# Attention, MoE and soft MoE on one core: q and k of batches 1 to 3 loaded in 32x32 blocks and transposed on VectorE

## Chip, core and metric

One core of a Trainium2 chip runs the kernel alone. The metric is the time of one execution in device microseconds (us), the median of several runs. Lower is better.

## What is computed

Three layers follow one another, all in float32: causal attention, a dense layer with a gated ReLU6, and a soft mixture of experts.

```python
batch, n_heads, seq, head_dim = 4, 12, 448, 64          # q, k, v

def _attn_ref(q, k, v):
    scores = np.matmul(q, k.transpose(0, 1, 3, 2)) / np.sqrt(64)
    scores = np.where(np.triu(np.ones((448, 448), bool), k=1), -1e9, scores)
    scores = scores - np.max(scores, axis=-1, keepdims=True)
    attn = np.exp(scores)
    attn = attn / (np.sum(attn, axis=-1, keepdims=True) + 1e-09)
    return np.matmul(attn, v)

def _moe_ref(x, w_in, w_out):                           # 1792 x 768, 768 x 2048, 2048 x 768
    h = x @ w_in
    return (h * np.clip(h + 3.0, 0.0, 6.0) / 6.0) @ w_out

def _moe2_ref(x, phi, w1, w2):                          # 8 experts of 4 slots, w1 8 x 768 x 1024
    logits = x @ phi
    d = softmax of logits over the 1792 tokens
    slot_input = (d.T @ x).reshape(8, 4, 768)
    slot_out[e] = np.maximum(slot_input[e] @ w1[e], 0.0) @ w2[e]
    return (softmax of logits over the 32 slots) @ slot_out
```

w_in and w_out arrive as 64-bit floats and are turned into 32-bit ones on the chip.

## The kernel before

**A planner writes the order.** Every piece of work is a `Step` with an engine (or several to choose from), a cost in us, the steps it depends on, the buffers it uses and a due time `prio`. `Schedule.run` places the steps one after the other: on each engine the step that can start first goes first, and among those that can start within `WAIT` of it the one with the smallest `prio`. Instructions are issued in that order, so each engine works through a fixed list. All DMAs are issued by SP (L398), so SP's list is the order of the transfers too. A buffer comes from a named pool and is given back after the last step that uses it. The constants in `TU` (L20) are due times, costs and buffer counts. Where the planner expects TensorE to idle it puts in filler matmuls (L382), whose result nobody reads.

**Attention** (L403) runs over 24 pairs of heads, six for each of the four batches. For a pair, two DMAs bring q into `qr` (112 partitions, four rows of 64 for each head) and two bring k into `kr`; there is one `qr` and one `kr` (`Q` is 1). Four TensorE transposes for each of them (L431, `tr`) put the head dimension onto the partitions, 448 columns in a PSUM buffer `t`. ScalarE copies that to `qp` or `kp` as the high part (L401), and VectorE subtracts it from the PSUM value for the low part (L437). From these come the scores with the mask (L453, L459), the row maxima on VectorE (L466), a diagonal matrix of the maxima on VectorE or GpSimd (L476 to L480), the scores again with the maxima taken off (L497, L502), exp on ScalarE (L512), the causal cut on GpSimd (L520), the product with v (L535), the division by the sums (L546 to L548), and a transpose of the result (L556) into `xp`, the input of the MoE. `xp` has two buffers, so batch 2 writes into the one that batch 0's MoE has left.

**The conversion** (`conv`, L573) of w_out (16 blocks, in the first stage) and w_in (16 blocks, while batch 0's MoE runs) loads 768 KB into `raw`, and ScalarE and VectorE put the 32-bit floats together (L577 to L589). The results go through the two `cx` buffers to DRAM (`wf_d`) and, split into high and low part (`wpl`, two buffers, L672 to L677), to `wi_d`. Later batches load them from there.

**The MoE** (L653) goes batch by batch over 16 units. Each unit multiplies `xp` with a block of w_in in 18 matmuls (L691), applies the gate (L696, L698), transposes the result through a PSUM buffer `t` (L705, L710), and from time to time feeds the logits (L720). There are two buffers `t`, and the transposes of attention, conversion and MoE share them.

**The experts** (L998, L1105) stream 50 MB of w1 and w2 through `ring` buffers. These come free in steps: after the conversion (`cv_end`), after attention (`a_end`), and as parts of the MoE end (`b_end` to `m_end`); `RINGS` says how many come at each step. The output is written at the end.

The change touches the attention of batches 1 to 3 up to `qp` and `kp`, and constants of the planner.

Of the kernel before, what the change touches and what calls it, by code (L numbers as in the profile page):

```python
# [9 lines left out]
F32 = mybir.dt.float32  # L10
# [8 lines left out]

TU = {'PO': [0.0, -5.47, -45.9, 12.37], 'TO': [-7.42, -0.39, 42.22, 1.8], 'PB': 0.11, 'AB': -0.28, 'TB': 293.74, 'DUTY': 0.6, 'RINGS': [3, 3, 2, 3, 1, 6, 2, 3], 'LOOK': 0.46, 'FILL': 0.96, 'RAW': 3, 'CA': 1, 'CW': 1, 'S': 2, 'PAIR': 15.8, 'UNIT': 3.58, 'WP0': 12.63, 'WPS': 9.72, 'T0': 82.6, 'L0': 11.83, 'L1': 5.94, 'GP': 244.34, 'TP': 7.98, 'ZP': 104.14, 'UP': -1.93, 'P0': 13.95, 'NQ': 2, 'WAIT': 0.12, 'AHEAD': 1.43, 'LAT': 0.23, 'CX': 2, 'G': 5, 'R': 1, 'VR': 2, 'XT': 2, 'Q': 1, 'AS': 1.42, 'A1': -3.91, 'A2': 3.39, 'A3': 15.18, 'A4': 12.3, 'A5': 11.1, 'A6': 20.26, 'A7': 6.65, 'DG': 2}  # L20

# [16 lines left out]
class Schedule:  # L38
# [4 lines left out]
    LAT = 0.15  # L43
    LATS = {"PE": 0.2, "ACT": 0.15, "DVE": 0.15, "POOL": 0.08, "SP": 0.1}
    LOOK = TU["LOOK"]
    BIAS = {"POOL": TU["PB"], "ACT": TU["AB"]}
    TB = TU["TB"]
# [138 lines left out]
def kernel(  # L186
# [12 lines left out]
    nc = tc.nc  # L199
# [68 lines left out]
    with tc.manual_schedule():  # L268
# [72 lines left out]
        nc.vector.memset(oner.bitcast(F32), 1.0)  # L341
        many(atp, TU["Q"], "qr", [112, QR, 2, DH])
        many(atp, TU["Q"], "kr", [112, QR, 2, DH])
        for t in many(atp, TU["VR"], "vr", [P, 2, NT, VD]):
# [52 lines left out]
        def dma(out, in_):  # L397
            nc.sync.dma_start(out=out, in_=in_)  # L398
# [4 lines left out]
        def attention(i):  # L403
# [7 lines left out]
            hs = slice(2 * hp, 2 * hp + 2)  # L411

            def ld(buf, src):
                for h in range(2):
                    dma(buf.t[:, :, h, :], src[b, 2 * hp + h].rearrange("(r p) d -> p r d", r=QR))

# [6 lines left out]
            for nm, buf, src in (("q", qr, q), ("k", kr, k)):  # L423
                l = sc.load(0.46e6, lambda buf=buf, src=src: ld(buf, src), [], [buf], p0 - 30, 2)
                tp, dst = sc.buf("t"), sc.buf(nm + "p")
                pl[nm] = dst

                def tr(tp=tp, buf=buf):
                    for r in range(QR):
                        x = buf.t[:, r].rearrange("p h d -> p (h d)")  # L430
                        nc.tensor.transpose(tp.t[:, 112 * r:112 * r + 112], x, ident[:112, :112])  # L431

                a = sc.add("PE", 0.5, tr, [l], [tp, buf, dst], p0)
                a.weight = 0.3
                c = sc.add("ACT", 0.58, lambda tp=tp, dst=dst: act_copy(dst.t[:, 0], tp.t[:, :S]), [a], [tp, dst], p0)
                his.append(c)
                los.append(sc.add("DVE", 0.61, lambda tp=tp, dst=dst: nc.vector.tensor_sub(  # L437
                    dst.t[:, 1], tp.t[:, :S], dst.t[:, 0].bitcast(F32)), [c], [tp, dst], p0))
            vl = sc.load(0.46e6, ldv, [], [vr], p0 - 20, 3)
# [4 lines left out]
            for part in (((3, 64), (0, 0)), ((1, 0), (2, 192))):  # L444
# [24 lines left out]

                a = sc.add("PE", 0.95, score, his, [ps, mc_, pl["q"], pl["k"]], P1)  # L470
                a.weight = 0.7
# [11 lines left out]

            d = sc.any([("POOL", 2.6, lambda: diag(nc.gpsimd)), ("DVE", 1.1, lambda: diag(nc.vector))], ms, [mc_, dg], P3)

# [53 lines left out]

            w = sc.add("PE", 2.1, pv, es + [vl], [o, s, vr], P6)  # L540
            w.weight = 0.6
# [31 lines left out]
        def conv(src, out, use, deps, prio, tag):  # L573
            raw, ca, cw = sc.buf("raw"), sc.buf("ca"), sc.buf("cw")
            l = sc.load(0.79e6, lambda: dma(raw.t.rearrange("p k f t -> p k (f t)"), src), [], [raw], prio - 12)
            hw = lambda: raw.t[:, :, :, 1]
            a = sc.add("ACT", 0.91, lambda: nc.scalar.activation(  # L577
                out=ca.t, in_=hw().bitcast(F32), func=ACTF.Copy, scale=2.0 ** -112), [l], [raw, ca], prio)
            c = sc.any([
                ("DVE", 0.74, lambda: nc.vector.tensor_scalar(  # L580
                    out=cw.t, in0=raw.t[:, :, :, 0].bitcast(U32), scalar1=29, scalar2=None,
                    op0=ALU.logical_shift_right)),
                ("ACT", 0.9, lambda: nc.scalar.activation(
                    out=cw.t, in_=raw.t[:, :, :, 0].bitcast(U32), func=ACTF.Copy, scale=LOW, bias=LOWB)),
            ], [l], [raw, cw], prio)
            e = sc.add("DVE", 1.04, lambda: nc.vector.scalar_tensor_tensor(  # L586
                out=cw.t, in0=ca.t.bitcast(U32), scalar=3, in1=cw.t,
                op0=ALU.logical_shift_left, op1=ALU.bitwise_or), [a, c], [ca, cw], prio)
            return sc.add("DVE", 1.06, lambda: nc.vector.scalar_tensor_tensor(  # L589
                out=out().bitcast(U32), in0=hw().bitcast(U32), scalar=0x80000000, in1=cw.t,  # L590
                op0=ALU.bitwise_and, op1=ALU.bitwise_or), [e] + deps, [raw, cw] + use, prio)
# [61 lines left out]
        for b in range(B):  # L653
# [5 lines left out]
            for ft in range(KF):  # L659
# [53 lines left out]

                a = sc.add("PE", 0.45, tr, [gg], [tp, g, gtb], pr - TU["TP"])
                a.weight = 0.35
# [482 lines left out]
```

## Time and profile before

| | us |
|---|---|
| median of 3 runs (687.77 to 694.6) | 690.55 |
| profiled execution, its time | 688.96 |
| profiled execution, its span | 687.2 |

The profile is of one execution on the chip. Its page begins with the busy time of each engine and closes with the groups of instructions and the DMA issues. PE is TensorE, PEld its weight loads, DVE VectorE, ACT ScalarE, POOL GpSimd, SP the engine that issues DMAs. The trace behind the page also answers questions: the busy time of all engines or of one line in stretches of time; the chain of waits, followed back from the last instruction, in order of time; groups of instructions by line and form with their mean duration; the DMA queue in a stretch; SP's own timeline. A share of the DMA engines is the mean busy share of the 16, by the time of their packets, and can go a little over 1 where packets overlap.

### The profile page before, as it was taken

What the parts mean: (1) busy time and instruction counts of PE and PEld (TensorE: products, weight loads), DVE (VectorE), ACT (ScalarE), POOL (GpSimd) and SP (SyncE); (2) the same over time, 40 slices, a digit from 0 to 9 for tenths busy, and PEclk for the clock granted to TensorE, in tenths of its full rate; (3) what the DMA queues carried; (4) which work ended last, traced back from release to release, by engine and by line L of the source; (5) the groups of instructions that cost most, each with busy time, mean ns of one, the idle gap of its engine ahead of it and who ended that gap; (6) DMA issues with size and microseconds to landing.
All of it is one profiled execution on the core that took longest, in us unless ns stands there. A gap on an engine that the chain in (4) does not pass through costs nothing.

```text
span 687.2 us, 16051 instructions
## 1 busy us (share of the span) xinstructions
PE 639.8 (93%) x6810; PEld 493.5 (72%) x6810; DVE 321.0 (47%) x658; ACT 265.6 (39%) x492; POOL 65.9 (10%) x131
## 2 busy tenths in 40 slices
PE   7898999999999999999999999999999999968374
PEld 5776888888888878888887888878698744522133
DVE  6786898878774544233445442123433333111101
ACT  2585665565653323333333233323344312201011
POOL 0231222224130000000000000000000010000000
PEclk7999999999999999999999999999999999996657
DMA  8889789999978935544543534279922399999997
GB/s 207 280 284 282 236 247 329 289 351 331 319 274 284 313 95 147 158 126 121 138 149 97 149 107 138 93 247 346 325 71 92 116 354 385 377 371 334 308 309 225
DMA packets 142614, 161.56 MB, mean 235 GB/s; under 512 B 71632, under 2 KB 113872, under 8 KB 142544
## 3 DMA queue, kind: packets, MB, share of 16 engines
q1 hardware_dynamic: 142544, 160.56, 72.6%
q8 instruction: 53, 0.87, 0.5%
q14 instruction: 17, 0.14, 0.1%
HBM read 129.86 MB, written 30.67 MB: 234 GB/s over the span
## 4 chain that ended last, share of the span: by engine, by line
PE 80%; DMA 12%; SPq 2%; DVE 2%; ACT 2%; issue 1%; ACTq 0%; DVEq 0%
PE ph L691 22%; PE pl L691 12%; PE o L535 7%; PE ps L497 6%; PE t L705 4%; DMA ring<-in_moe_w_dram 4%; PE ps L453 3%; PE t L431 3%; PE t L556 3%; SPq L398 2%; DMA raw<-in_moe_w_out_dram 2%; DMA wos<-in_moe_w_dram 2%; PE t L619 2%; PE ps L459 2%; PE ps L502 2%; PE t L849 2%
## 5 line engine op out<-in xcount | busy, mean ns | idle before, releaser
L691 PE MATMUL ph<-xp,wpl 128*128 128x448 f32 x720 | 157.1, 371 | 0.8 <-DMA wpl<-wi_d 0.8
L691 PEld LDWEIGHTS ph<-xp,wpl 128*128 128x128 f32 x720 | 132.2, 188 | 17.0 <-ACT r L696 2.2
L691 PE MATMUL pl<-xp,wpl 128*128 128x448 f32 x432 | 94.3, 371 | 0.9 <-DMA wpl<-wi_d 0.9
L691 PEld LDWEIGHTS pl<-xp,wpl 128*128 128x128 f32 x432 | 79.5, 188 | 7.9 <-DMA wpl<-wi_d 1.2
L520 POOL TENSOR_SCALAR_AFFINE_SELECT s<-s 128x256 f32<-128x256 f32 x96 | 42.9, 470 | 340.1 <-ACT s L512 287.1
L698 DVE SCALAR_TENSOR_TENSOR g<-r,ph 128x448 f32<-128x448 f32 x40 | 24.8, 621 | 100.7 <-ACT r L696 100.7
L696 ACT ACTIVATE r<-ph,three 128x448 f32<-128x448 f32 x40 | 25.3, 634 | 104.0 <-PE ph L691 104.0
L466 DVE TENSOR_REDUCE mc<-ps 128x2 f32<-128x896 f32 (+1 forms) x96 | 61.4, 682 | 5.8 <-PE ps L459 4.9
L512 ACT ACTIVATE s<-ps 128x896 f32<-128x896 f32 (+2 forms) x72 | 50.2, 732 | 27.2 <-PE ps L502 26.3
L497 PE MATMUL ps<-qp,kp 64*64 64x64 f32 (+3 forms) x576 | 57.5, 306 | 2.0 <-ACT s L512 2.0
L497 PEld LDWEIGHTS ps<-qp,kp 64*128 64x128 f32 (+1 forms) x576 | 41.9, 174 | 17.2 <-issue 8.8
L535 PE MATMUL o<-vr,s 128*64 128x65 f32 (+1 forms) x1536 | 53.6, 224 | 0.0
L535 PEld LDWEIGHTS o<-vr,s 128*64 128x64 f32 (+1 forms) x1536 | 48.6, 137 | 3.6 <-issue 1.0
L710 ACT ACTIVATE gtok<-t 128x384 f32<-128x384 f32 x64 | 31.0, 485 | 29.8 <-PE t L705 29.7
L705 PE MATMUL t<-ident,g 128*128 128x128 f32 (+1 forms) x256 | 39.2, 280 | 0.0
L698 DVE SCALAR_TENSOR_TENSOR g<-r,pl 128x448 f32<-128x448 f32 x24 | 14.9, 620 | 50.5 <-ACT r L696 50.4
L586 DVE SCALAR_TENSOR_TENSOR cw<-ca,cw 128x768 uint32<-128x768 uint32 x32 | 33.3, 1040 | 10.2 <-ACT ca L577 5.2
L577 ACT ACTIVATE ca<-raw 128x768 f32<-128x768 f32 x32 | 29.2, 912 | 21.8 <-DMA raw<-in_moe_w_in_dram 7.3
L696 ACT ACTIVATE r<-pl,three 128x448 f32<-128x448 f32 x24 | 15.2, 634 | 52.6 <-PE pl L691 52.6
L453 PE MATMUL ps<-kp,qp 64*128 64x448 f32 (+1 forms) x192 | 34.6, 362 | 0.7 <-ACT kp L401 0.3
L705 PEld LDWEIGHTS t<-ident,g 128*128 128x128 f32 (+1 forms) x256 | 26.8, 133 | 8.0 <-issue 1.2
L1113 PE MATMUL o<-ring,wos 128*32 128x128 f32 (+1 forms) x248 | 20.4, 449 | 11.5 <-DMA ring<-in_moe_w_dram 11.5
(208 smaller groups left out, 823.1 us busy)
## 6 DMA issues: line engine op xcount, KB each, us to landing
ring<-in_moe_w_dram SPq DMA_DIRECT2D x44, 768.0 KB, 10.9
wpl<-wi_d SPq DMA_DIRECT2D x32, 768.0 KB, 4.4
raw<-in_moe_w_out_dram SPq DMA_DIRECT2D x16, 768.0 KB, 6.0
raw<-in_moe_w_in_dram SPq DMA_DIRECT2D x16, 768.0 KB, 7.5
wi_d<-wpl SPq DMA_DIRECT2D x16, 768.0 KB, 6.1
ring<-in_moe_w_dram SPq DMA_DIRECT2D x22, 512.0 KB, 8.5
wo_d<-gtok SPq DMA_DIRECT2D x16, 384.0 KB, 3.9
wf_d<-cx SPq DMA_DIRECT2D x16, 384.0 KB, 7.0
```

Of the source, the lines that this page charges most:

```text
L453: nc.tensor.matmul(ps.t[:n, h, c:c + w], pl["q"].t[r, 0, q0:q0 + n], pl["k"].t[r, 0, 0:w], start=(t == part[0][0]), stop=False, skip_group ...
L466: nc.vector.tensor_reduce(out=mc_.t[:n, 2 * t - 1:2 * t + 1] if t else mc_.t[:n, 0:8:7], in_=ps.t[:n, :, c:c + q0 + n], axis=AX.X, op=ALU. ...
L497: nc.tensor.matmul(ps.t[:kn, h, col:col + n], pl["k"].t[r, x, q0:q0 + kn], pl["q"].t[r, y, q0:S], start=(c == 0 and col == 0), stop=False, ...
L512: nc.scalar.activation(out=o, in_=x, func=ACTF.Exp, scale=SCALE)
L520: nc.gpsimd.affine_select(out=x, in_=x, pattern=[[0, 2], [1, kn]], compare_op=ALU.is_ge, fill=0.0, base=0, channel_multiplier=-1)
L535: nc.tensor.matmul(o.t[64 * h:64 * h + 64, VD * j:VD * j + VD], s.t[:kn, h, c:c + 64], vr.t[:kn, h, t, :], start=(t == 0), stop=(t == ts[- ...
L586: e = sc.add("DVE", 1.04, lambda: nc.vector.scalar_tensor_tensor(out=cw.t, in0=ca.t.bitcast(U32), scalar=3, in1=cw.t, op0=ALU.logical_shif ...
L691: nc.tensor.matmul(h.t[:, :S], w.t[:, a, kk, :], x.t[:, c, kk, :], start=(n == 0), stop=(n == len(seq) - 1))
L696: rr = sc.add("ACT", 0.63, lambda h=h, r=r: nc.scalar.activation(out=r.t, in_=h.t[:, :S], func=ACTF.Relu, bias=three), [hh], [h, r], pr - ...
L698: gg = sc.add("DVE", 0.62, lambda h=h, r=r, g=g: nc.vector.scalar_tensor_tensor(out=g.t, in0=r.t, scalar=6.0, in1=h.t[:, :S], op0=ALU.min, ...
L705: nc.tensor.transpose(tp.t[:n, t * P:(t + 1) * P], g.t[:, t0:t0 + n], ident)
L710: nc.scalar.activation(out=gflat[:, :3 * DFF].rearrange("p (t f) -> p t f", f=DFF)[:, :, c], in_=v3[:, 0:3, :], func=ACTF.Copy)
```

## The change

For the pairs of batches 1 to 3 (`i >= DV`, 6), q and k are loaded in blocks. A head's 448 x 64 values are cut into 14 x 2 blocks of 32 x 32. Each of four DMAs (two heads, two halves of the head dimension) fills 32 partitions: partition p gets from each of the 14 blocks its row p, 32 values, side by side. One VectorE instruction for q and one for k then transposes each 32x32 block in place of the four TensorE transposes, from `qr` or `kr` to one of two new SBUF buffers `tt`. ScalarE's copy and the subtraction read `tt` instead of PSUM, and the subtraction may be placed on GpSimd. Batch 0 keeps the TensorE transposes.

Besides, constants of the planner change: costs of a few steps; due times (`P0`, `WP0`, `L0`, `UNIT`, `A1`, `A2`, `A3`, `A5`, `UP`); the weights by which it chooses engines (`AB`, `LOOK`, `TB`); `AHEAD`, how far a load may be issued before the planner expects the DMA queue to be free; and one of the ring buffers is handed out after the conversion instead of at the start.

```diff
-TU = {... 'AB': -0.28, 'TB': 293.74, 'RINGS': [3, 3, 2, 3, 1, 6, 2, 3], 'LOOK': 0.46, 'UNIT': 3.58, 'WP0': 12.63, 'L0': 11.83, 'UP': -1.93, 'P0': 13.95, 'AHEAD': 1.43, 'A1': -3.91, 'A2': 3.39, 'A3': 15.18, 'A5': 11.1, ...}
+TU = {... 'AB': -0.76, 'TB': 218.28, 'RINGS': [2, 4, 2, 3, 1, 6, 2, 3], 'LOOK': 0.89, 'UNIT': 5.16, 'WP0': 14.31, 'L0': 1.9, 'UP': -2.35, 'P0': 12.93, 'AHEAD': 6.71, 'A1': -3.2, 'A2': 5.94, 'A3': 19.21, 'A5': 18.36, ..., 'DV': 6, 'TT': 2, 'LO': 2.57}
...
-        many(atp, TU["Q"], "qr", [112, QR, 2, DH])
-        many(atp, TU["Q"], "kr", [112, QR, 2, DH])
+        many(atp, TU["Q"], "qr", [P, 512])
+        many(atp, TU["Q"], "kr", [P, 512])
+        many(atp, TU["TT"], "tt", [P, S])
...
+            blocks = i >= TU["DV"]
+
             def ld(buf, src):
                 for h in range(2):
-                    dma(buf.t[:, :, h, :], src[b, 2 * hp + h].rearrange("(r p) d -> p r d", r=QR))
+                    if not blocks:
+                        dma(buf.t[:112, :].rearrange("p (r h d) -> p r h d", r=QR, h=2)[:, :, h, :],
+                            src[b, 2 * hp + h].rearrange("(r p) d -> p r d", r=QR))
+                    for c in range(2 * blocks):
+                        r = 64 * h + 32 * c
+                        dma(buf.t[r:r + 32, :S].rearrange("p (n d) -> p n d", d=32),
+                            src[b, 2 * hp + h, :, 32 * c:32 * c + 32].rearrange("(n p) d -> p n d", p=32))
...
-                l = sc.load(0.46e6, lambda buf=buf, src=src: ld(buf, src), [], [buf], p0 - 30, 2)
-                tp, dst = sc.buf("t"), sc.buf(nm + "p")
+                l = sc.load(0.46e6, lambda buf=buf, src=src: ld(buf, src), [], [buf], p0 - 30, 4 if blocks else 2)
+                tp, dst = sc.buf("tt" if blocks else "t"), sc.buf(nm + "p")
...
-                a = sc.add("PE", 0.5, tr, [l], [tp, buf, dst], p0)
+                if blocks:
+                    a = sc.add("DVE", 0.62, lambda tp=tp, buf=buf: nc.vector.transpose(tp.t, buf.t[:, :S]), [l], [tp, buf, dst], p0)
+                else:
+                    a = sc.add("PE", 0.5, tr, [l], [tp, buf, dst], p0)
...
-                los.append(sc.add("DVE", 0.61, lambda tp=tp, dst=dst: nc.vector.tensor_sub(
-                    dst.t[:, 1], tp.t[:, :S], dst.t[:, 0].bitcast(F32)), [c], [tp, dst], p0))
+                lo = [("DVE", 0.61, lambda tp=tp, dst=dst: nc.vector.tensor_sub(
+                    dst.t[:, 1], tp.t[:, :S], dst.t[:, 0].bitcast(F32)))]
+                if blocks:
+                    lo.append(("POOL", 1.2, lambda tp=tp, dst=dst: nc.gpsimd.tensor_sub(
+                        dst.t[:, 1], tp.t, dst.t[:, 0].bitcast(F32))))
+                los.append(sc.any(lo, [c], [tp, dst], p0 + (TU["LO"] if blocks else 0.0)))
...
-                a = sc.add("PE", 0.95, score, his, [ps, mc_, pl["q"], pl["k"]], P1)
+                a = sc.add("PE", 0.77, score, his, [ps, mc_, pl["q"], pl["k"]], P1)
...
-            d = sc.any([("POOL", 2.6, lambda: diag(nc.gpsimd)), ("DVE", 1.1, lambda: diag(nc.vector))], ms, [mc_, dg], P3)
+            d = sc.any([("POOL", 2.1, lambda: diag(nc.gpsimd)), ("DVE", 1.27, lambda: diag(nc.vector))], ms, [mc_, dg], P3)
```

The costs of three more steps change: the product with v from 2.1 to 2.16, the shift of a conversion on VectorE from 0.74 to 0.58, and the transposes of a MoE unit from 0.45 to 0.47.

## Rows read from the trace of the kernel before

**Rows 1.** The page: span; busy us (share of the span) and instructions.

```profile
span 687.2 us, 16051 instructions
...
PE 639.8 (93%) x6810; PEld 493.5 (72%) x6810; DVE 321.0 (47%) x658; ACT 265.6 (39%) x492; POOL 65.9 (10%) x131
```

**Rows 2.** Stages: us; PE, PEld, DVE, ACT, POOL busy (instructions); clock; DMA; GB/s.

```profile
0.00:106.00 106.00, 95.54 (x1353) 76.70 (x1353) 82.50 (x158) 60.20 (x95) 21.89 (x49) 0.94 0.84 256
106.00:240.00 134.00, 133.84 (x1505) 114.24 (x1504) 97.18 (x170) 71.55 (x126) 26.68 (x37) 1.00 0.95 312
240.00:455.00 215.00, 215.00 (x2368) 180.76 (x2367) 84.56 (x197) 75.00 (x152) 15.51 (x44) 1.00 0.42 128
455.00:552.00 97.00, 95.27 (x534) 77.45 (x536) 31.51 (x49) 39.10 (x81) 0.00 (x0) 1.00 0.59 203
552.00:640.00 88.00, 74.89 (x814) 31.99 (x806) 19.78 (x74) 14.46 (x32) 1.81 (x1) 0.92 1.04 365
640.00:687.00 47.00, 25.26 (x248) 12.40 (x248) 5.43 (x11) 5.30 (x11) 0.00 (x0) 0.61 0.98 281
```

**Rows 3.** The same stages, the filler matmuls of L382 alone, first two.

```profile
0.00:106.00 106.00, 17.71 (x104) 11.83 (x104) 0.94 0.84 256
106.00:240.00 134.00, 0.00 (x0) 0.00 (x0) 1.00 0.95 312
```

**Rows 4.** The chain in order of time: start us, us, what (four pieces).

```profile
127.70 0.92 PE t L431 x8
...
137.47 9.91 DMA wf_d<-cx
...
332.78 3.66 PE ph L691 x18
...
601.27 11.82 DMA ring<-in_moe_w_dram
```

**Rows 5.** Stages, the transposes of L431 alone.

```profile
0.00:106.00 106.00, 10.61 (x72) 7.89 (x72) 0.94 0.84 256
106.00:240.00 134.00, 6.91 (x51) 5.05 (x49) 1.00 0.95 312
240.00:455.00 215.00, 10.25 (x72) 7.43 (x72) 1.00 0.42 128
```

**Rows 6.** Groups by line and form: count, busy us, mean ns, idle.

```profile
L586 DVE SCALAR_TENSOR_TENSOR cw<-ca,cw 128x768 uint32<-128x768 uint32 x32 | 33.3, 1040 | 10.2 <-ACT ca L577 5.2 <-ACT cw L583 4.5
...
L437 DVE TENSOR_TENSOR qp<-t,qp 128x448 fp32r<-128x448 f32 x24 | 14.8, 618 | 23.1 <-ACT qp L401 23.1
...
L480 DVE TENSOR_TENSOR dg<-id,mc 128x448 fp32r<-128x448 f32 x20 | 12.5, 625 | 0.7
...
L480 POOL TENSOR_TENSOR dg<-id,mc 128x448 fp32r<-128x448 f32 x4 | 3.7, 936 | 0.3
```

**Rows 7.** DMA queue (packets, MB, share), 4.5:6.5 us, then 20:30 us.

```profile
q1 hardware_dynamic: 1525, 0.29, 72.8%
...
q1 hardware_dynamic: 3154, 2.09, 73.0%
```

**Rows 8.** DMA issues: out<-in, queue, count, KB each, median us to landing.

```profile
qr<-in_q_dram SPq DMA_DIRECT2D x48, 112.0 KB, 3.2
...
phis<-in_moe_phi_dram SPq DMA_DIRECT2D x1, 96.0 KB, 2.5
```

**Rows 9.** SP: q DMAs (min/median/max ns), then its timeline (start, us, what).

```profile
L398 SPq DMA_DIRECT2D qr<-in_q_dram x48: 313/481/1288, 0.8 to 383.6; - x48
...
105.87 0.86 SPq L398 DMA_DIRECT2D qr<-in_q_dram  x2
...
128.26 0.99 SPq L398 DMA_DIRECT2D qr<-in_q_dram  x2
129.34 1.41 SPq L398 DMA_DIRECT2D kr<-in_k_dram  x2
```

**Rows 10.** SP's timeline, the first ring load.

```profile
202.75 0.69 SPq L398 DMA_DIRECT2D ring<-in_moe_w_dram  x1
```

More of the change, by code (lines that the diff above doesn't have):

```diff
@@ L17 @@
 PSUM = bass.MemoryType.PSUM
-TU = {'PO': [0.0, -5.47, -45.9, 12.37], 'TO': [-7.42, -0.39, 42.22, 1.8], 'PB': 0.11, 'AB': -0.28, 'TB': 293.74, 'DUTY': 0.6, 'RINGS': [3, 3, 2, 3, 1, 6, 2, 3], 'LOOK': 0.46, 'FILL': 0.96, 'RAW': 3, 'CA': 1, 'CW': 1, 'S': 2, 'PAIR': 15.8, 'UNIT': 3.58, 'WP0': 12.63, 'WPS': 9.72, 'T0': 82.6, 'L0': 11.83, 'L1': 5.94, 'GP': 244.34, 'TP': 7.98, 'ZP': 104.14, 'UP': -1.93, 'P0': 13.95, 'NQ': 2, 'WAIT': 0.12, 'AHEAD': 1.43, 'LAT': 0.23, 'CX': 2, 'G': 5, 'R': 1, 'VR': 2, 'XT': 2, 'Q': 1, 'AS': 1.42, 'A1': -3.91, 'A2': 3.39, 'A3': 15.18, 'A4': 12.3, 'A5': 11.1, 'A6': 20.26, 'A7': 6.65, 'DG': 2}
+TU = {'PO': [0.0, -5.47, -45.9, 12.37], 'TO': [-7.42, -0.39, 42.22, 1.8], 'PB': 0.11, 'AB': -0.76, 'TB': 218.28, 'DUTY': 0.6, 'RINGS': [2, 4, 2, 3, 1, 6, 2, 3], 'LOOK': 0.89, 'FILL': 0.96, 'RAW': 3, 'CA': 1, 'CW': 1, 'S': 2, 'PAIR': 15.8, 'UNIT': 5.16, 'WP0': 14.31, 'WPS': 9.72, 'T0': 82.6, 'L0': 1.9, 'L1': 5.94, 'GP': 244.34, 'TP': 7.98, 'ZP': 104.14, 'UP': -2.35, 'P0': 12.93, 'NQ': 2, 'WAIT': 0.12, 'AHEAD': 6.71, 'LAT': 0.23, 'CX': 2, 'G': 5, 'R': 1, 'VR': 2, 'XT': 2, 'Q': 1, 'AS': 1.42, 'A1': -3.2, 'A2': 5.94, 'A3': 19.21, 'A4': 12.3, 'A5': 18.36, 'A6': 20.26, 'A7': 6.65, 'DG': 2, 'DV': 6, 'TT': 2, 'LO': 2.57}
 class Step:
@@ L429, in tr @@
                     for r in range(QR):
-                        x = buf.t[:, r].rearrange("p h d -> p (h d)")
-                        nc.tensor.transpose(tp.t[:, 112 * r:112 * r + 112], x, ident[:112, :112])
-                a = sc.add("PE", 0.5, tr, [l], [tp, buf, dst], p0)
+                        nc.tensor.transpose(tp.t[:, 112 * r:112 * r + 112], buf.t[:112, P * r:P * r + P], ident[:112, :112])
+                if blocks:
+                    a = sc.add("DVE", 0.62, lambda tp=tp, buf=buf: nc.vector.transpose(tp.t, buf.t[:, :S]), [l], [tp, buf, dst], p0)
+                else:
+                    a = sc.add("PE", 0.5, tr, [l], [tp, buf, dst], p0)
                 a.weight = 0.3
@@ L538, in pv @@
                             )
-            w = sc.add("PE", 2.1, pv, es + [vl], [o, s, vr], P6)
+            w = sc.add("PE", 2.16, pv, es + [vl], [o, s, vr], P6)
             w.weight = 0.6
@@ L579, in conv @@
             c = sc.any([
-                ("DVE", 0.74, lambda: nc.vector.tensor_scalar(
+                ("DVE", 0.58, lambda: nc.vector.tensor_scalar(
                     out=cw.t, in0=raw.t[:, :, :, 0].bitcast(U32), scalar1=29, scalar2=None,
@@ L712, in ev @@
                     nc.scalar.activation(out=gtok(3, ft * P, P)[1], in_=v3[0:64, 3, :], func=ACTF.Copy)
-                a = sc.add("PE", 0.45, tr, [gg], [tp, g, gtb], pr - TU["TP"])
+                a = sc.add("PE", 0.47, tr, [gg], [tp, g, gtb], pr - TU["TP"])
                 a.weight = 0.35
```

## The prediction

> **What bounds the kernel now.** The page comes first: in the profiled execution TensorE is busy for 639.8 of 687.2 us, VectorE for under half [rows 1]. That share averages over stages with different limits, so the second view is the table of stages [rows 2], cut where the chain of waits changes its kind, with the filler matmuls (L382, dummy work that the planner puts into TensorE's gaps) beside it [rows 3]. Five stages are to be seen. Up to 106 us (attention of batch 0, conversion of w_out) TensorE looks 90% busy, but 17.71 us of that is filler, so it isn't the bound. From 106 to 240 us (batch 0's MoE on freshly converted w_in, attention of batch 1) TensorE is full, without filler, and the DMA engines are busy for 0.95 of the time. From 240 to 455 us TensorE is full and DMA is at 0.42; from 455 to 552 us it is nearly full. From 552 us on (experts, output) DMA is at 1.04 and 0.98 and TensorE waits for it, 11.82 us long in one place [rows 4].
>
> The third view is the chain of waits in order of time [rows 4]. In the crowded stage the eight transposes of a pair stand on it for 0.92 us, and it also runs through a store of converted weights, 9.91 us long, that holds a cx buffer; after that stage it is TensorE's work, piece after piece. So between 106 and 240 us two resources are near their limit, and between 240 and 552 us one, TensorE.
>
> **What the change removes.** Eight TensorE transposes for each of 18 pairs (L431). By stage [rows 5]: 72 stand before 106 us, of which 48 belong to batch 0's six pairs, which keep them; 51 stand in the crowded stage and 72 after it. At 0.92 / 8 = 0.115 us each that is 51 x 0.115 = 5.9 us between 106 and 240 us and 72 x 0.115 = 8.3 us after it. The 24 before 106 us are worth nothing: the filler there shows that TensorE has time to spare. Where TensorE is full, each microsecond taken from it comes off the end, as the last stage begins when its MoE work is done: the 135 us from 552 to 687.2 us go by the bytes of the experts' weights, which the change leaves alone, so that stage shifts as a whole. The sum is 14.2 us.
>
> **What it adds on VectorE, ScalarE and GpSimd.** Two block transposes of 128x448 for each pair. No row shows that operation. The nearest have the same shape: the subtraction out of PSUM, 618 ns, and the multiplication out of SBUF, 625 ns [rows 6]. I take 0.6 us, and for the range nothing to double that, 1.2 us. In the crowded stage the seven pairs add 14 x 0.6 = 8.4 us to VectorE's 97.18 of 134 us (14 x 1.2 = 16.8 us at double) [rows 2], which leaves room at either end. The subtraction for the low part now reads SBUF and may go to GpSimd, where the multiplication of this shape takes 936 ns [rows 6], on an engine busy for 26.68 of 134 us. ScalarE's copy stays. What is new is the place in VectorE's queue: a transpose stands behind conversions of 1.04 us each [rows 6], and the scores of that pair wait behind it. I cost this at nothing, since TensorE has a MoE unit of some 3.7 us, such as the one at 332.78 us [rows 4], to do meanwhile; without that cover it would be about one conversion for each load, 14 x 1.04 = 14.6 us in the stage. The tt buffers also free the two PSUM buffers t of two uses for each pair, which can only help the MoE's transposes; I count nothing.
>
> **What it adds on DMA.** A q or k load was 896 runs of 256 B in two DMAs; it becomes 1792 runs of 128 B in four. Two stretches with different mean sizes give the price of a run [rows 7]. 1525 packets and 0.29 MB (190 B each) took 72.8% of 16 engines for 2 us, 15.3 ns each; 3154 packets and 2.09 MB (663 B) took 73.0% for 10 us, 37.0 ns. The line through both is 6.5 ns and 0.046 ns for each byte: 18.3 ns for 256 B and 12.4 ns for 128 B. A load then goes from 896 x 18.3 / 16 = 1.02 us of all engines to 1792 x 12.4 / 16 = 1.39 us, 0.36 us more. The bounds are nothing (bytes alone count) and 1.02 us (a short run costs as much as a long one). The one load in 128 B runs, phis with 768 of them, landed in 2.5 us, no later than a q DMA of 448 runs with its 3.2 us [rows 8], so I stay by the line. Seven pairs in the crowded stage make 14 x 0.36 = 5.1 us (0 to 14.3 us), against a share of 0.05 x 134 = 6.7 us that is free there. It just fits. After 240 us there is room for any of these prices.
>
> One rule speaks against the change. The Trainium skill (DMA: Bandwidth & Descriptors, How a descriptor splits into AXI transactions) says that a read starts from a multiple of 256 B, and that one whose data begin later also fetches what lies before them and pays for it; a right half begins 128 B into its row. By the rows, which know no such difference, the sum stays at 14.2 us; by the rule it would be 5.3 us, an estimate that the first rival below works out as a mechanism of this kernel.
>
> **Issue.** Each load has two more DMAs on SP, 0.48 us each by the median, and two took 1.41 us where the queues were full [rows 9]. SP issues in order, so the stores of converted weights stand behind them, and conversions wait for those. The sum counts nothing, as SP has gaps between its issues in which the extra ones fit; the upper end is 1.41 us for each load and is the rival on the other side. The queues of ACT and GpSimd issue no DMA.
>
> **The new constants** (priorities, costs, AHEAD, one ring later) change the planner's order, not the work. In the stage up to 106 us they could win part of the 17.71 us of filler, or lose as much; where TensorE is full an order gives nothing. I take 0, since batch 0's pairs and the conversion keep their work, and a third, 6 us, either way for the range. The ring that comes later is not missed: the first ring load of the profile starts at 202.7 us [rows 10], about where the conversion ends and the ring is handed over.
>
> **The rivals.**
> *Batch 0's MoE goes by DMA.* If a right half costs what a 256 B run costs, a load is 896 x (12.4 + 18.3) / 16 = 1.72 us, 0.69 us more, and the stage gets 14 x 0.69 = 9.7 us, 3.0 more than is free. Then the 5.9 us of the crowded stage don't come off, it grows by 3.0 us, and the gain is 8.3 - 3.0 = 5.3 us: 683.7 us. For it: the store on the chain. Against it: phis. The rule of the Trainium skill named above asks for this case.
> *Every run costs the same.* 14.3 us less the 6.7 us that are free is 7.6 us, against 8.3 us gained later: 688.3 us, no change to be seen. Against it is the slope between the two stretches.
> *VectorE's queue.* Without the cover of MoE units the 14.6 us above take back the 14.2 us: 689.4 us. Against it: VectorE is idle for a quarter of the crowded stage [rows 2].
> *A better order early.* The filler of the first stage shrinks by a third too: 14.2 + 6 = 20.2 us, 668.8 us.
> *SP's queue (slower).* Each of the 14 loads of the crowded stage holds up the store behind it by 1.41 us, and the stage grows by 14 x 1.41 = 19.7 us; less 8.3 us it is 11.4 us slower, 700.4 us. It decides from 8.3 / 14 = 0.59 us for each load on. For it: the store on the chain is issued by that queue. Against it: the q loads of two pairs are issued at 105.87 and 128.26 us [rows 9], which leaves SP long stretches between them.
>
> **How the numbers follow.** The profiled execution took 688.96 us, 1.76 us more than its span and 1.59 us less than the median, 690.55 us, of runs from 687.77 to 694.6 us. 688.96 - 14.2 = 674.8 us, and on the scale of the median 676 us, which is the forecast; its own range is 671 to 681 us (0.36 us for each of the 14 loads either way). The rivals on the same scale: 685.3, 689.9, 691, 670.4 and 702 us. Chances: forecast 0.52, DMA with dear right halves 0.14, every run alike 0.07, VectorE's queue 0.05, better order 0.13, SP's queue 0.09. This measurement can tell about 1% from no change, so faster means under 683.6 us and slower over 697.5 us. Faster: 0.52 + 0.13 and half of the dear right halves, 0.72. Slower: SP's queue and a little of the rest, 0.10. Same: 0.18. The range from 664 to 690 us leaves out SP's queue, half of the equal runs and of VectorE's queue, and the far end of the better order, some 0.18.
>
> **What would show it.** Right: 48 transposes on L431 instead of 192; TensorE still full without filler from the start of batch 0's MoE to the end of batch 3's; that stretch, now 446 us, about 14 us shorter; the last stage as long as before, 135 us; VectorE's block transpose near 0.6 us; some 32,000 more packets under 512 B with the DMA share under 1 after the crowded stage. Wrong: filler or waits of TensorE between 106 and 240 us (then the transport or SP), a q or k load landing many microseconds later with TensorE waiting on qp or kp, a last stage longer than 135 us, or a first stage that moves by more than 6 us.

## The result

The changed kernel took 683.89 us in the median (679.13 to 685.78, 12 runs), the kernel before 691.34 us (12 runs). The ratio is 0.988 with a 95% interval of 0.985 to 0.991: about 8 us faster, a little over 1%. The forecast was 676 us. The sign is right and the time lies in the range, but the gain is little more than half of what was forecast, and the experiments show that it is not the forecast's sum that came out a bit small: it is what three terms of 1 to 2% each leave over, two of which the sum had at nothing.

### The profile page after: what moved, and what is told of

Read it like the earlier page. It is cut to its first block, busy times and chain, and to the rows that moved or that the text cites. A ratio compares the mean times of both kernels' runs of the same rounds, so it can differ in the third digit from the quotient of the medians.

```text
span 682.1 us, 15907 instructions
## 1 busy us (share of the span) xinstructions
PE 631.6 (93%) x6656; PEld 483.1 (71%) x6656; DVE 337.8 (50%) x668; ACT 264.4 (39%) x490; POOL 98.1 (14%) x159
## 2 busy tenths in 40 slices
DMA packets 176024, 161.58 MB, mean 237 GB/s; under 512 B 105040, under 2 KB 147280, under 8 KB 175952
## 4 chain that ended last, share of the span: by engine, by line
PE 67%; DMA 18%; DVE 8%; ACT 3%; issue 2%; SPq 1%; POOL 0%; DVEq 0%; ACTq 0%
PE ph L706 20%; PE pl L706 10%; PE o L550 6%; DMA raw<-in_moe_w_out_dram 5%; PE ps L512 4%; PE t L720 4%; DMA ring<-in_moe_w_dram 4%; DMA raw<-in_moe_w_in_dram 3%; PE ps L468 2%; PE t L571 2%; DMA wos<-in_moe_w_dram 2%; PE t L864 2%; PE ph L1030 2%; PE ps L1030 1%; SPq L399 1%
## 5 line engine op out<-in xcount | busy, mean ns | idle before, releaser
L706 PE MATMUL ph<-xp,wpl 128*128 128x448 f32 x738 | 162.7, 374 | 0.0
L706 PEld LDWEIGHTS ph<-xp,wpl 128*128 128x128 f32 x738 | 136.8, 190 | 16.2 <-issue 1.8
L535 POOL TENSOR_SCALAR_AFFINE_SELECT s<-s 128x256 f32<-128x256 f32 x96 | 49.2, 536 | 289.9 <-ACT s L527 272.9
L706 PE MATMUL pl<-xp,wpl 128*128 128x448 f32 x414 | 90.3, 371 | 0.0
L706 PEld LDWEIGHTS pl<-xp,wpl 128*128 128x128 f32 x414 | 76.1, 188 | 8.0 <-issue 1.5
L550 PE MATMUL o<-vr,s 128*64 128x65 f32 (+1 forms) x1536 | 56.8, 231 | 0.9 <-POOL s L535 0.9
L550 PEld LDWEIGHTS o<-vr,s 128*64 128x64 f32 (+1 forms) x1536 | 51.4, 143 | 5.3 <-issue 1.6
L592 ACT ACTIVATE ca<-raw 128x768 f32<-128x768 f32 x32 | 29.5, 921 | 33.6 <-DMA raw<-in_moe_w_out_dram 18.9
L713 DVE SCALAR_TENSOR_TENSOR g<-r,pl 128x448 f32<-128x448 f32 x23 | 14.2, 619 | 50.6 <-ACT r L711 50.6
L468 PEld LDWEIGHTS ps<-kp,qp 64*128 64x128 f32 x192 | 17.8, 179 | 21.4 <-ACT s L527 9.6
```

Of the source, the lines that this page charges most:

```text
L468: nc.tensor.matmul(ps.t[:n, h, c:c + w], pl["q"].t[r, 0, q0:q0 + n], pl["k"].t[r, 0, 0:w], start=(t == part[0][0]), stop=False, skip_group ...
L535: nc.gpsimd.affine_select(out=x, in_=x, pattern=[[0, 2], [1, kn]], compare_op=ALU.is_ge, fill=0.0, base=0, channel_multiplier=-1)
L550: nc.tensor.matmul(o.t[64 * h:64 * h + 64, VD * j:VD * j + VD], s.t[:kn, h, c:c + 64], vr.t[:kn, h, t, :], start=(t == 0), stop=(t == ts[- ...
L706: nc.tensor.matmul(h.t[:, :S], w.t[:, a, kk, :], x.t[:, c, kk, :], start=(n == 0), stop=(n == len(seq) - 1))
L713: gg = sc.add("DVE", 0.62, lambda h=h, r=r, g=g: nc.vector.scalar_tensor_tensor(out=g.t, in0=r.t, scalar=6.0, in1=h.t[:, :S], op0=ALU.min, ...
```

## The profile after

The page, then two of the stages of [rows 2] (us; busy time of PE, PEld, DVE, ACT, POOL with instructions; clock; DMA share; GB/s):

```profile
span 682.1 us, 15907 instructions
...
DMA packets 176024, 161.58 MB, mean 237 GB/s; under 512 B 105040, under 2 KB 147280, under 8 KB 175952
```

```profile
106.00:240.00 134.00, 126.80 (x1364) 104.16 (x1363) 96.75 (x165) 69.50 (x123) 41.77 (x45) 0.99 0.91 285
240.00:455.00 215.00, 214.99 (x2306) 181.18 (x2306) 99.26 (x221) 76.74 (x154) 17.80 (x46) 1.00 0.52 147
```

The late stage is what was forecast: from 240 to 455 us TensorE is full and DMA, at 0.52, has room. The crowded stage has not: TensorE is busy for 126.80 of 134 us, where it had 133.84 [rows 2], so 7 us of idle time have come into the stage in which it was the bound, while VectorE (96.75 us) is where it was. There are 176,024 packets, 33,410 more than before, close to the 32,256 that twice the runs in 36 loads make, and the DMA share in the crowded stage has fallen, from 0.95 to 0.91, as have the GB/s, from 312 to 285. That is not a resource that has run full.

What moved is read best from three marks: the start of the first MoE matmul, the end of the last one, and the end of the span. They come from the MoE's matmul line (count, min/median/max ns, first and last start in us), here of the kernel before and of the changed one:

```profile
L691 PE MATMUL ph<-xp,wpl x720: 358/365/475, 106.5 to 548.8; 128*128 128x448 f32 x180
...
L691 PE MATMUL pl<-xp,wpl x432: 358/365/714, 116.4 to 543.7; 128*128 128x448 f32 x144
```

```profile
L706 PE MATMUL ph<-xp,wpl x738: 358/368/721, 109.3 to 547.1; 128*128 128x448 f32 x185
...
L706 PE MATMUL pl<-xp,wpl x414: 358/368/477, 114.3 to 542.0; 128*128 128x448 f32 x138
```

With 0.37 us for the last matmul the MoE ran from 106.5 to 549.2 us before (442.7 us) and from 109.3 to 547.5 us after (438.2 us); what follows took 138.0 us before and 134.6 us after. So of the 5.1 us between these two spans (the medians are some 8 us apart) 4.5 came from the MoE stretch (14 were forecast), 3.4 from the last stage (none was forecast), and the start lost 2.8.

The waits (who waited for what: us in total, times, longest) name the place, ahead of the crowded stage and in it:

```profile
ACT ca L592 <- DMA raw<-in_moe_w_out_dram: 18.9, 9, 4.0
...
DVE cw L595 <- DMA raw<-in_moe_w_in_dram: 11.2, 4, 3.4
ACT ca L592 <- DMA raw<-in_moe_w_in_dram: 9.2, 3, 4.3
```

Up to 108 us ScalarE waits 18.9 us for blocks of w_out, and from 108 to 240 us VectorE and ScalarE wait 20.4 us for blocks of w_in. In the kernel before ScalarE's waits were these:

```profile
ACT ca L577 <- DMA raw<-in_moe_w_out_dram: 7.2, 4, 3.3
...
ACT ca L577 <- DMA raw<-in_moe_w_in_dram: 6.0, 3, 4.0
```

The conversion's loads come late though the DMA engines move less. SP's own timeline shows what they stand behind (start us, us, what; the loads of two pairs, after the change):

```profile
62.99 2.53 SPq L399 DMA_DIRECT2D qr<-in_q_dram  x4
65.62 6.20 SPq L399 DMA_DIRECT2D kr<-in_k_dram  x4
...
80.80 3.25 SPq L399 DMA_DIRECT2D qr<-in_q_dram  x4
84.15 3.39 SPq L399 DMA_DIRECT2D kr<-in_k_dram  x4
```

Such a row runs from the start of its first DMA to the end of its last, waits between them included. The eight DMAs of one pair's q and k hold SP for 8.7 us and for 6.6 us. Before the change a pair's four took 2.4 us [rows 9]. All other transfers are in the same list and wait.

## The experiments

All times are medians against the kernel before on the same chip (691 to 695 us there). The three marks are from one profiled execution of each and scatter by some us: the changed kernel and its two copies with other columns (below), the same instructions in the same order, start the MoE at 109.3, 113.3 and 113.8 us.

| kernel | ratio to before (95%) | MoE starts | MoE lasts | after it |
|---|---|---|---|---|
| before | 1 | 106.5 | 442.7 | 138.0 |
| changed | 0.988 (0.985 to 0.991) | 109.3 | 438.2 | 134.6 |
| constants alone | 0.979 (0.975 to 0.983) | 102.6 | 443.0 | 131.3 |
| blocks alone | 0.992 (0.989 to 0.996) | 111.2 | 434.4 | 138.2 |
| 256 B runs, two DMAs | 0.969 (0.965 to 0.973) | 103.3 | 432.6 | 134.0 |
| 256 B runs, four DMAs | 0.980 (0.975 to 0.984) | 109.5 | 434.1 | 134.0 |
| 128 B runs, two DMAs | 0.978 (0.973 to 0.983) | 108.4 | 435.6 | 134.1 |
| transposes twice | 0.988 (0.983 to 0.993) | 115.3 | 438.9 | 132.4 |
| left halves | 0.984 (0.979 to 0.989) | 113.3 | 437.0 | 134.0 |
| right halves | 0.990 (0.983 to 0.996) | 113.8 | 437.0 | 134.1 |
| blocks late | 0.968 (0.963 to 0.972) | 102.9 | 433.5 | 133.6 |
| AHEAD alone | 0.994 (0.991 to 0.998) | 105.9 | 447.4 | 132.5 |
| constants without AHEAD | 1.003 (0.999 to 1.007) | 109.9 | 442.2 | 141.1 |
| loads by GpSimd's queue | 0.980 (0.975 to 0.985) | 109.3 | 433.4 | 132.5 |

**The two halves of the change.** First the constants without the blocks, and the blocks without the constants.

```diff
-TU = {... 'DV': 6, ...}        # of the changed kernel
+TU = {... 'DV': 24, ...}
```

> The changed kernel with all pairs on TensorE transposes (DV 24): the new constants alone. Three theories for the part of the gain that is missing in the crowded stage (106 to 240 us), where TensorE idles for about 7 us after the change. Transport (short runs and more DMAs delay w_in): the constants are neutral, so about the time before, 688 to 692 us, TensorE full again in the crowded stage. Constants (the new due times reorder the crowded stage): idle TensorE there stays, 690 to 697 us. VectorE's queue: as transport, 688 to 692 us. The 3.4 us by which the last stage got shorter (138.0 to 134.6 us from the end of the MoE to the end) show here if they come from the constants.

Measured: 679.61 us, 14 us faster than before. None of the theories had said this. The constants, put at nothing in the forecast, win nearly twice what the whole change wins, and blocks on top of them lose. ScalarE's waits up to 108 us and from there to 240 us, the row of the crowded stage, the MoE line, and SP's loads of two pairs:

```profile
ACT ca L592 <- DMA raw<-in_moe_w_out_dram: 15.9, 8, 3.9
...
ACT ca L592 <- DMA raw<-in_moe_w_in_dram: 5.8, 4, 3.1
...
106.00:240.00 134.00, 134.00 (x1517) 112.21 (x1515) 89.60 (x158) 67.53 (x121) 27.80 (x41) 1.00 0.85 285
...
L706 PE MATMUL ph<-xp,wpl x720: 358/367/711, 102.6 to 540.0; 128*128 128x448 f32 x180
...
L706 PE MATMUL pl<-xp,wpl x432: 358/365/472, 109.2 to 545.2; 128*128 128x448 f32 x144
...
63.75 1.60 SPq L399 DMA_DIRECT2D qr<-in_q_dram  x2
65.45 0.99 SPq L399 DMA_DIRECT2D kr<-in_k_dram  x2
...
91.67 1.67 SPq L399 DMA_DIRECT2D qr<-in_q_dram  x2
93.43 3.40 SPq L399 DMA_DIRECT2D kr<-in_k_dram  x2
```

TensorE is full in the crowded stage, the MoE stretch is as long as before (443.0 us), but it starts 3.9 us earlier and the last stage is 6.7 us shorter. A pair's q and k hold SP for 2.6 and 5.1 us. ScalarE waits for w_out nearly as long as in the changed kernel (15.9 us against 18.9), and yet the MoE starts 6.7 us earlier, so that wait does not tell what delays the start. The wait that comes with the blocks is the one for w_in: 5.8 us for ScalarE and 1.0 us for VectorE here, 9.2 and 11.2 us in the changed kernel.

```diff
-TU = {...}                     # of the changed kernel, and its costs
+TU = {... as before ..., 'DV': 6, 'TT': 2, 'LO': 2.57}
```

> The block loads and VectorE transposes with all constants and costs of before: the change in the data path alone. Transport or VectorE's queue: TensorE idles in the crowded stage, only the late 8.3 us are gained and the last stage stays at 138 us: 681 to 685 us. Constants: the full 14 us, 675 to 679 us.

Measured: 688.41 us, 5 us faster than before and slower than either range. The crowded stage, the same for the filler matmuls alone, and the MoE line:

```profile
106.00:240.00 134.00, 129.58 (x1428) 107.78 (x1425) 102.50 (x169) 73.54 (x125) 24.49 (x44) 1.00 0.87 269
...
106.00:240.00 134.00, 5.71 (x42) 4.10 (x42) 1.00 0.87 269
...
L706 PE MATMUL ph<-xp,wpl x720: 358/366/711, 111.2 to 545.2; 128*128 128x448 f32 x180
```

The MoE stretch is shorter by 8.3 us, as much as the late share of the forecast (72 transposes of 0.115 us), the start is 4.7 us later, and the last stage stays at 138.2 us. TensorE idles for 4.4 us of the crowded stage and runs filler for 5.7 us, which together is more than the 5.9 us that the transposes gave back there, so the 8.3 us do not measure the late share alone. So the shorter last stage belongs to the constants, and the late start and the lost time of the crowded stage belong to the blocks.

The two halves do not add up: -2.1% and -0.8% would make -2.9%, and the change has -1.2%. On the kernel before the blocks win 5 us, on the new constants they lose 6. SP's k DMAs from 60 to 240 us (min/median/max ns) show a difference, first with the old constants, then in the changed kernel:

```profile
L399 SPq DMA_DIRECT2D kr<-in_k_dram x40: 317/478/1761, 73.1 to 233.3; - x40
...
L399 SPq DMA_DIRECT2D kr<-in_k_dram x36: 470/987/2718, 65.6 to 239.7; - x36
```

The same DMA holds SP twice as long, by the median, with the new constants; which of them does it is not shown.

**What in the blocks costs.** The same order and the same VectorE work, but loads in fewer and longer runs:

```diff
-                    for c in range(2 * blocks):
-                        r = 64 * h + 32 * c
-                        dma(buf.t[r:r + 32, :S].rearrange("p (n d) -> p n d", d=32),
-                            src[b, 2 * hp + h, :, 32 * c:32 * c + 32].rearrange("(n p) d -> p n d", p=32))
+                    if blocks:
+                        dma(buf.t[64 * h:64 * h + 64, :S].rearrange("p (n d) -> p n d", d=64),
+                            src[b, 2 * hp + h].rearrange("(n p) d -> p n d", p=64))
```

> The changed kernel in the same order, but each head's q or k comes in one DMA of 64 partitions with 256 B runs (7 blocks of 64 x 64, so the scores are of rearranged values): half the runs and half the DMAs, same bytes, VectorE work unchanged. Transport: 4 to 7 us faster than the changed kernel, 677 to 680 us. Constants or VectorE's queue: within 1.5 us of it, 683 to 685 us.

Measured: 671.89 us. Against the ratio of the changed kernel that is 0.969 to 0.988, 13 us, twice what was expected: transport is the cost, and it is about as large as the 14.2 us that the forecast gave TensorE. SP's timeline, the crowded stage and the MoE line:

```profile
61.17 1.55 SPq L399 DMA_DIRECT2D qr<-in_q_dram  x2
62.83 1.48 SPq L399 DMA_DIRECT2D kr<-in_k_dram  x2
...
106.00:240.00 134.00, 130.26 (x1413) 107.82 (x1413) 98.50 (x167) 70.81 (x123) 40.62 (x43) 1.00 0.93 298
...
L705 PE MATMUL ph<-xp,wpl x738: 358/368/711, 103.3 to 535.5; 128*128 128x448 f32 x185
```

A pair's q and k now hold SP for 3.0 us, the MoE starts at 103.3 us, near the 102.6 us of the constants alone, and TensorE is busy for 130.26 us of the crowded stage. The MoE stretch, 432.6 us, is 10.4 us shorter than with the constants alone: 14.2 us less the 3.7 us that TensorE still idles in that stage.

VectorE instead, each transpose written twice (`[nc.vector.transpose(...) for _ in range(2)]`):

> The changed kernel with each block transpose done twice: 36 more VectorE instructions of 0.62 us, 12 of them in the crowded stage (7.4 us) and 20 after it. VectorE's queue: most of the 7.4 us shows, 689 to 692 us. Transport or constants: VectorE is idle for a quarter of the crowded stage and takes it, 684 to 686 us.

Measured: a ratio of 0.988, that of the changed kernel. The 7.4 us of more work in the crowded stage would be 1.1%, and the two intervals together leave no room for all of it. VectorE's queue falls as the main cost.

**Runs or DMAs.** The two cells between: four DMAs of 256 B runs, and two DMAs of 128 B runs.

```diff
-                            src[b, 2 * hp + h, :, 32 * c:32 * c + 32].rearrange("(n p) d -> p n d", p=32))
+                            src[b, 2 * hp + h, 224 * c:224 * c + 224].rearrange("(n p) d -> p n d", p=32))
```

> As the kernel with two DMAs of 256 B runs for each load (the same order, scores of rearranged values), but in four DMAs of 32 partitions: run size as before the change, number of DMAs as after it. If the 13 us that those loads gave back were the time SP needs for twice the DMAs, most of it is lost again: 682 to 686 us, and SP is held for 6 to 9 us by a pair's q and k. If they were the runs of 128 B: 671 to 675 us.

```diff
-                        dma(buf.t[64 * h:64 * h + 64, :S].rearrange("p (n d) -> p n d", d=64),
-                            src[b, 2 * hp + h].rearrange("(n p) d -> p n d", p=64))
+                        dma(buf.t[64 * h:64 * h + 64, :S].rearrange("p (n d) -> p n d", d=32),
+                            src[b, 2 * hp + h].rearrange("s (c d) -> (s c) d", d=32).rearrange("(n p) d -> p n d", p=64))
```

> The other half of that pair: 128 B runs as in the changed kernel, but in two DMAs of 64 partitions for each load (scores of rearranged values). If the number of DMAs costs: 671 to 675 us. If the number of runs costs, by the engines or by SP's issue: 682 to 686 us.

Both lie halfway, at 679.11 and 678.01 us, where neither expectation had put them. From 0.969, twice the DMAs add 0.011 and twice the runs add 0.009, and both together the 0.019 that separate the changed kernel from it: the two prices add up, some 7 us and 6 us. Each ratio is good to half a percent, so that they add up exactly is luck. SP's timeline, a pair's k in four DMAs of 256 B runs and in two of 128 B runs:

```profile
66.47 4.06 SPq L399 DMA_DIRECT2D kr<-in_k_dram  x4
...
64.42 5.29 SPq L399 DMA_DIRECT2D kr<-in_k_dram  x2
```

With the pair's q, either alone holds SP for 7 us, where it had been 3.0. But the two do it in different ways. With two DMAs of 128 B runs each is long, 2.6 us. With four of 256 B runs they are short, and SP waits between them (60 to 240 us: the k DMAs, then the two longest of SP's waits for transfers):

```profile
L399 SPq DMA_DIRECT2D kr<-in_k_dram x36: 311/398/1084, 66.5 to 235.5; - x36
...
SPq L399 <- DMA raw<-in_moe_w_in_dram: 9.4, 5, 3.7
...
SPq L399 <- DMA ring<-in_moe_w_dram: 5.3, 4, 2.4
```

The program gives SP's DMAs eight semaphores in turn, so one cannot be issued before the one eight places ahead of it has landed. In this run SP waits 26 us for landings, 24 us of it inside the loads of q and k; with two DMAs of 128 B runs and in the changed kernel it is less than 1 us. So twice the DMAs hold SP because they reach back sooner to a large transfer that has not landed, and twice the runs because each issue takes longer.

The DMA engines' time tells the two apart as well (queue, packets, MB, share of 16 engines over the span), 256 B runs in two DMAs, then in four:

```profile
q1 hardware_dynamic: 142544, 160.56, 73.8%
...
q1 hardware_dynamic: 143696, 160.56, 73.0%
```

0.738 x 669.9 x 16 = 7910 us and 0.730 x 677.6 x 16 = 7914 us: the 7 us for twice the DMAs aren't the engines'. The changed kernel has 0.748 x 682.1 x 16 = 8163 us. For the runs, the engines' time therefore stays a rival beside the longer issue.

**Where a run starts.** Both halves of a load read the left 32 columns, or both the right ones:

```diff
-                            src[b, 2 * hp + h, :, 32 * c:32 * c + 32].rearrange("(n p) d -> p n d", p=32))
+                            src[b, 2 * hp + h, :, 0:32].rearrange("(n p) d -> p n d", p=32))
```

> The changed kernel, but both halves of a load read the left 32 columns, so that every run of 128 B starts at a multiple of 256 B in DRAM (scores of the wrong columns). By the rule that a run starting 128 B later also costs the bytes before it: half the runs get 5.9 ns cheaper, 0.33 us for each load, 3 to 5 us faster than the changed kernel, 680 to 682 us. Without that difference: within 1.5 us of it, 684 to 687 us.

> The changed kernel, but both halves of a load read the right 32 columns, so that every run of 128 B starts 128 B behind a multiple of 256 B (scores of the wrong columns). By the rule that such a start also costs the bytes before it: 3 to 5 us slower than the changed kernel, 687 to 691 us, and some 180 x 16 us more in the DMA engines' time than with left halves alone. Without that difference: 682 to 686 us, and the engines' time within 1% of both.

Measured: 682.47 us (0.984) and 686.69 us (0.990), with intervals that overlap; the time alone doesn't settle a difference of 4 us. The DMA engines' own time does (queue, packets, MB, share of 16 engines over the span), left halves first, then right halves:

```profile
q1 hardware_dynamic: 175952, 160.56, 74.8%
...
q1 hardware_dynamic: 175952, 160.56, 75.2%
```

0.748 x 684.3 x 16 = 8190 us against 0.752 x 684.9 x 16 = 8241 us: 51 us, 0.6%, over the 64,512 runs of the 36 loads. The rule of the first rival asked for 5.9 ns a run, 381 us (the "180 x 16 us" of the expectation is a slip). Two kernels with equal packets, the one before and the constants alone, differ by more than the 51 us (0.726 x 687.2 x 16 = 7983 us and 0.725 x 676.9 x 16 = 7852 us), but by a third of the 381.

**A version from it.** Blocks only for batches 2 and 3 (`'DV': 12`), where for the most part the queue has room, with the new constants:

> The changed kernel with the blocks only for batches 2 and 3 (DV 12), so that the first stage and most of the crowded one keep TensorE transposes and 256 B runs, and the new constants stay. If the transport costs only where the DMA queue is full: faster than the constants alone (679.6 us) by what TensorE saves late, 8 to 11 us: 669 to 672 us. If it costs everywhere: 676 to 682 us.

Measured: 671.07 us, a ratio of 0.968, as expected. It beats both kernels, by 23 us and by some 14 us.

```profile
106.00:240.00 134.00, 134.00 (x1510) 112.70 (x1510) 96.35 (x171) 69.64 (x125) 27.73 (x41) 1.00 0.89 290
...
L706 PE MATMUL ph<-xp,wpl x846: 358/368/714, 102.9 to 536.0; 128*128 128x448 f32 x170
```

TensorE is full through the crowded stage, and from 240 to 455 us as well (214.99 of 215 us). The MoE stretch is 9.5 us shorter than with the constants alone, for 96 transposes that at 0.115 us make 11.0 us. The blocks of four pairs are still loaded between 173 and 240 us, in the crowded stage; TensorE is full there all the same, and where in that stage the room begins is not shown.

**Which constant.** AHEAD alone in the kernel before (`'AHEAD': 6.71`), and all new constants but it:

> The kernel before with one constant of the change, AHEAD 6.71 in place of 1.43. The constants alone gave 14 us; in their trace the last stage is 131.3 us instead of 138.0 (ring loads no longer stand in SP's list behind output stores that wait) and the MoE starts 3.9 us earlier. If AHEAD does the one or both: the last stage 131 to 133 us, in all 680 to 688 us. If it is due times and weights: 692 to 695 us as before.

> The counterpart: all pairs on TensorE transposes, all new constants but AHEAD, which stays at 1.43. If AHEAD makes the last stage shorter: the last stage is back at 137 to 139 us, and what is left of the 14 us is the share of the due times, 685 to 690 us in all. If the due times do it: 679 to 682 us.

Measured: 689.48 and 694.90 us. AHEAD does shorten the last stage, from 138.0 to 132.5 us, and without it that stage is long again (141.1 us). The whole table agrees: 138.0 to 141.1 us in the three kernels with the old AHEAD, 131.3 to 134.6 us in the eleven with the new one. SP's timeline tells why, here at the end of the kernel before and then of the constants alone:

```profile
624.02 3.28 SPq L398 DMA_DIRECT2D wos<-in_moe_w_dram  x2
633.06 2.37 SPq L398 DMA_DIRECT2D out_dram<-wos  x2
...
638.77 2.83 SPq L398 DMA_DIRECT2D out_dram<-wos  x2
641.68 28.25 SPq L398 DMA_DIRECT2D ring<-in_moe_w_dram  x17
```

```profile
623.83 6.10 SPq L399 DMA_DIRECT2D ring<-in_moe_w_dram  x4
630.02 2.36 SPq L399 DMA_DIRECT2D out_dram<-wos  x2
632.48 8.30 SPq L399 DMA_DIRECT2D ring<-in_moe_w_dram  x5
640.89 2.55 SPq L399 DMA_DIRECT2D out_dram<-wos  x2
643.54 17.93 SPq L399 DMA_DIRECT2D ring<-in_moe_w_dram  x9
```

Before, after two loads at 624.02 us SP's next entries are output stores that have to wait for their data until 633.06 and 638.77 us, and 17 ring loads stand behind them. With the larger AHEAD nine ring loads go out ahead of and between those stores. That is the expected effect on the last stage; but AHEAD alone gives only 0.6%, since its MoE stretch is 4.7 us longer, and the other constants alone give nothing, which neither expectation had. Together they give 2.1%. That much of the gain comes from both in one plan is shown; by which of the due times it does is not, and stays open.

**SP's part, taken away.** The block loads go through GpSimd's queue:

```diff
-                        dma(buf.t[r:r + 32, :S].rearrange("p (n d) -> p n d", d=32),
-                            src[b, 2 * hp + h, :, 32 * c:32 * c + 32].rearrange("(n p) d -> p n d", p=32))
+                        nc.gpsimd.dma_start(out=buf.t[r:r + 32, :S].rearrange("p (n d) -> p n d", d=32),
+                            in_=src[b, 2 * hp + h, :, 32 * c:32 * c + 32].rearrange("(n p) d -> p n d", p=32))
```

> The changed kernel, same order, but GpSimd's queue issues the block loads of q and k in place of SP's. If the time lost is SP being held by them (6 to 9 us for a pair where the queue is full) while loads and stores of the conversion wait behind: the MoE starts at 102 to 105 us instead of 109 and the whole takes 673 to 679 us. If it is the DMA engines' time for the runs themselves: 682 to 687 us as the changed kernel. If issuing holds GpSimd so long that the diagonal and the cut come late, it is slower than that.

Measured: 677.61 us, a ratio of 0.980 against 0.988 for the changed kernel, some 6 us, as expected in all; but the MoE starts no earlier (109.3 us), and the gain is in the MoE stretch (433.4 us) and the last stage. So it speaks for SP's part in the crowded stage and leaves the first stage open. It isn't a clean cut either: GpSimd is busy for 51.12 of the first 106 us, against 35.29 in the changed kernel, and the runs go differently on that queue:

```profile
q1 hardware_dynamic: 109136, 152.29, 68.9%
q0 software_dynamic: 4608, 8.27, 4.9%
```

64,512 runs became 4608 packets there, 14 runs each, in 0.049 x 675.2 x 16 = 529 us of the engines' time, 8.2 ns for a run.

## Why the forecast was right, and where it was not

**The number: right in sign and range, partly by luck.** 683.89 us lies in the wide range, which holds four of the six cases that were weighed, and outside the forecast's own, 671 to 681 us. It is nearest to the rival with dear right halves, 685.3 us, whose mechanism the engines' time does not bear out. The gain is what is left of terms that were not in the sum.

**TensorE's gain: right late, lost in the crowded stage.** Where only the late pairs have blocks, 9.5 of 11.0 us came off; with the old constants the MoE stretch was 8.3 us shorter. The 5.9 us of the crowded stage did not come off: TensorE idles there. The step that failed is "It just fits": a share of free engine time was taken as free transport.

**The price of a run: about right, and beside the point.** With long runs in the same order the engines took 7910 us, in the changed kernel 8163 us: 253 us or 0.44 us of all 16 engines for each of 36 loads, where 0.36 was forecast. Against the kernel before, in another order, it is 180 us or 0.31. Both are far from the 1.02 us of the rival in which every run costs the same. What the loads cost is 13 us of the kernel's time, and it comes about half from the number of DMAs, which had been put at nothing because "SP has gaps between its issues in which the extra ones fit". The mis-sized term is the hold: 1.41 us was taken from two DMAs in a full queue as the upper end, and a pair's eight took 6.6 and 8.7 us where its four took 2.4 to 5.1. Two DMAs of 128 B runs held SP as long as four of 256 B, the ones by their issue, the others by the wait for an earlier landing, which the forecast did not have.

**The rivals.** SP's queue was the one that was there, with its place and its mechanism, conversion loads late behind q and k. Its size was not: the kernel did not become 11 us slower, and with the old constants, the case that it was worked out for, the blocks still win 5 us. Blocks also delay the first stage, where the forecast had seen only TensorE's spare time: they move the MoE's start by 4.7 us with the old constants and by 6.7 us with the new ones, with the scatter named above. That it is transport there too is shown by the long runs in two DMAs (103.3 us); that it is SP's hold is not, as the start stays at 109.3 us with GpSimd's queue. Dear right halves, named with the rule of the Trainium skill (DMA: Bandwidth & Descriptors, How a descriptor splits into AXI transactions), are not borne out: the engines' time differs by 51 us between left and right halves, where the rule asked for 381 us. VectorE's queue falls with the doubled transposes. The better order early is there in part: the constants win in the first stage, but more in the last.

**VectorE's work: right.** 0.6 us was forecast; the rows of the changed kernel (count, busy us, mean ns, idle) have 637 and 603 ns:

```profile
L442 DVE STREAM_TRANSPOSE tt<-qr 128x448 f32<-128x448 f32 x18 | 11.5, 637 | 0.0
L442 DVE STREAM_TRANSPOSE tt<-kr 128x448 f32<-128x448 f32 x18 | 10.9, 603 | 0.0
```

**The constants: wrong, and the largest miss.** The step "where TensorE is full an order gives nothing. I take 0" looked only at stages in which TensorE is the bound. The constants work on SP's list: in the last stage it decides which ring loads stand behind waiting stores. How they win in the first stage is not shown. "That stage shifts as a whole" failed for the same reason: the bytes of the last stage are the same, but SP doesn't always have a load to issue. A first stage that moved by less than 6 us was to have meant that the constants do nothing there; it moved by 2.8 us because 3.9 us gained and 6.7 us lost lay on top of each other. The 3.9 us are within the scatter of single executions, but the kernel with late blocks, which loads its first twelve pairs as the constants alone do, has the same start (102.9 us).

In the sum: constants -2.1%, TensorE's work with long runs -1.0% (0.969 against 0.979), transport +1.9% (0.988 against 0.969), -1.2% in all. The split holds for this order, constants first; taken the other way, the blocks are -0.8% and the constants -0.4%.

## What to carry to other kernels

Where one queue issues all transfers in order, price a finer load by the time for which it holds that queue when it is full, by the earlier transfers whose landing it must await, and by what stands behind it, not by the engines' free share. When a change comes with new constants of a planner, ask of each queue, not only of the busiest engine, what it will now do earlier. And put such work where its feed has room: with the same constants, blocks in the late batches took 8 us off, and blocks everywhere put 6 us on.

## What was not expected of the hardware

A block transpose of 128x448 in float32 takes 0.60 to 0.64 us on VectorE, as long as a subtraction of that shape. A k DMA of 448 runs of 128 B held SP for 0.99 us in the median (changed kernel, 60 to 240 us), one of 224 runs of 256 B, the same bytes in the same order, for 0.40 us. 128 B runs that start 128 B behind a multiple of 256 B took no more of the DMA engines' time than aligned ones, within what equal kernels scatter. GpSimd's queue put the 14 runs of a partition into one packet and needed 8.2 ns of engine time for a run, where 12.4 ns were estimated from [rows 7] for SP's.
